# An mLSTM and mixer kernel: the first batch's weight staging, conversions and second token products put in another order

## The chip, the cores and the metric

The kernel runs on one core of one Trainium2 chip. Its engines are TensorE (PE; its weight loads are shown apart as PEld), VectorE (DVE), ScalarE (ACT), GpSimd (POOL) and SyncE (SP), which issues most of the DMAs. The metric is the device time of one execution in microseconds. TensorE's clock has two levels, 1.2 and 2.4 GHz; the profile shows the granted clock as a share of 2.4 GHz.

## The reference, cut to what matters

```python
for t in range(S):                      # B, H, S, D = 4, 8, 768, 40
    m_new = max(f[t] + m, i[t])
    f_stab, i_stab = exp(f[t] + m - m_new), exp(i[t] - m_new)
    C = f_stab * C + i_stab * outer(v[t], k[t])
    n = f_stab * n + i_stab * k[t]
    y[t] = sigmoid(o[t]) * (C @ q[t]) / max(abs(n . q[t]), 1)
x = y.transpose(0, 2, 1, 3).reshape(B, S, 320)
u = x + (relu(x^T @ w_tok1) @ w_tok2)^T     # token mixing: 768 -> 256 -> 768
out = u + relu(u @ w_ch1) @ w_ch2           # channel mixing: 320 -> 1536 -> 320
```

## The kernel before

The sequence is cut into NC = 6 chunks of 128 tokens; a unit is (batch, chunk). Within a chunk the recurrence becomes matrix products: scores `ps_sc` (`st_s`), weighted by exponentials `dd` (`prep_exp`, from a PSUM tile `ps_phi` for batch 0), times `v` (`st_pv`, tile `po`), plus the carried state `Cn` times the scaled queries `q3t` (`st_state`). `x0_ops` turns `po` into the mixer's input `x` and its two fp32r halves `xh`, `xl`.

The mixer's matmuls run in fp32r, each operand as a high and a low half. The weights come as 64-bit words in 30 pieces of 384 columns: pieces 0 to 3 are `w1`, 4 to 7 `w2`, then pairs of `c1` and `c2` in turn (8, 9 = `c1`; 10, 11 = `c2`; 12, 13 = `c1`; ...). A piece is loaded into a staged buffer `wst` (`dec_load`, SP). `dec_abs` makes its exponent part `pf` (ACT, in PSUM) and its low word (ACT, or GpSimd for even pieces once `early` is off). `dec_ops` joins them on DVE (two instructions a piece: `pf`, then `wf`). `dec_hi` (ACT) rounds `wf` to the high half, `dec_low` (GpSimd) subtracts for the low half. `wst` has four buffers in the pool `wq`, and three more in `wx` once `sp` is released.

Batch 0 goes chunk by chunk in a loop of five turns, c = 1 to 5; "turn 3" is the pass with c = 3, and u5 is the last unit of batch 0. Each turn does the scores of the next unit, the state and values of its own, and the decoding of two pieces. After the loop come the first token product (`a_part`, tile `ps_a`; `a_end` makes `rh`, `rl`), eleven small transposes of the gate sums (`cols`, tile `gt`, from `w_row`, which `rows_w` makes on GpSimd), the second token products (`phase_b`, six, tile `ps_b`), their transposes (`phase_t`, six), and then 18 slots: `gemm1` (16 products into `ps_h`; ACT makes `gh`, DVE `gl`) and, one slot late, `gemm2` (12 products into `acc`). Slots 0 to 10 of batch 0 also decode a pair of pieces each. Batches 1 to 3 follow with the attention of the next batch laced into the slots.

The order of instructions on each engine is the order of the code; semaphores set the rest. Every matmul of the mixer has one line, that of `mm3`, so stages are told apart by tiles. PSUM has eight banks: two each for `ps_h`, `acc`, `ps_s` and `ps_m`.

Of the kernel before, what the change touches and what calls it, by code (L numbers as in the profile page):

```python
# [25 lines left out]
HP = 9  # L26
# [8 lines left out]
def kernel(ctx: ExitStack, tc: tile.TileContext, gates, qk, q3, kv, og,  # L35
                            wt1, wt2, wc1, wc2, ident, out):
    nc = tc.nc
# [70 lines left out]
    floor_b = wp.tile([128, 1], F32, name="floor_b")  # L108
    nc.gpsimd.memset(floor_b, 2.0 ** -14 - 0.5)
    phi, b_t = z[0:B * HP, 0], z[0:B * HP, 1]  # L110
    w_row = pp.tile([B * HP, NC - 1, L], F32, name="w_row")
    phi_d = dp.tile([NC, B * HP, L], F32, name="phi_d")
    bcol = wp.tile([128, NC, B * HP], F32, name="bcol")
    wcol = wp.tile([128, NC, B * HP], F32, name="wcol")
# [28 lines left out]
                             t.rearrange("p (i g) -> p i g", i=3), AF.Exp)  # L143

    def rows_w():
        p = phi.rearrange("p (c t) -> p c t", t=L)[:, 0:NC - 1, L - 1:L]
        nc.gpsimd.tensor_tensor(w_row, b_t[:, 0:(NC - 1) * L].rearrange("p (c t) -> p c t", t=L),
                                p.to_broadcast([B * HP, NC - 1, L]), ALU.add)

    def cols():  # L150
        t = ps_m.tile([128, 2 * NC - 1, B * HP], F32, tag="m", name="gt")
        e = id_t[0:B * HP, 0:B * HP]
        for c in range(NC - 1):
            nc.tensor.transpose(t[:, c], w_row[:, c], e)
        for c in range(NC):
            nc.tensor.transpose(t[:, NC - 1 + c], b_t[:, c * L:(c + 1) * L], e)
        nc.scalar.activation(wcol[:, 0:NC - 1, :].rearrange("p c (b g i) -> p (c b) i g", b=B, g=3),
                             t[:, 0:NC - 1].rearrange("p c (b i g) -> p (c b) i g", b=B, g=3), AF.Exp)
        nc.vector.tensor_copy(bcol, t[:, NC - 1:])

    def spread_late(pool, tag):
        ps = pool.tile([128, 4, L], F32, tag=tag, name="ps_phi")
# [444 lines left out]
    def dec_load(n):  # L607
        while nxt[0] < min(n, len(pieces)):
            d, w, a = pieces[nxt[0]]
            late = wx and (nxt[0] - wx[1]) % 7 < 3  # L610
            t = (wx[0] if late else wq).tile([128, WP, 2], I32, tag="wst", name="wst", bufs=3 if late else 4)
            nc.sync.dma_start(out=t.rearrange("p n t -> p (n t)"), in_=w[:, a:a + WP].bitcast(I32))
            staged[nxt[0]] = t
            nxt[0] += 1
# [77 lines left out]
    def phase_b(b, s, pool=(ps_m, "m")):  # L692
        rh, rl = R[b]
        ps = pool[0].tile([128, DM], F32, tag=pool[1], name="ps_b")
        t = []
        for j in range(2):
            a = slice(j * S + s * 128, j * S + (s + 1) * 128)
            t += [(w2[0][:, a], rh[:, j, :]), (w2[1][:, a], rh[:, j, :]), (w2[0][:, a], rl[:, j, :])]
        mm3(ps, [t[i] for i in (0, 1, 3, 4, 2, 5)], True, True)
        x = xs[(b, s)][0]  # L700
        nc.vector.tensor_tensor(x, ps, x, ALU.add)
        xd = lp.tile([128, 2, 64], F32, tag="xd", name="xd", bufs=3)
        nc.vector.tensor_copy(xd, x[:, 256:320].unsqueeze(1).to_broadcast([128, 2, 64]))
# [51 lines left out]
    def step(g, n=1):  # L755
        for _ in range(n):
            next(g, None)

    def warm(n, pool=(ps_m, "m"), z=zero):
        t = pool[0].tile([128, 512], F32, tag=pool[1], name="warm")  # L760
        for i in range(n):
            nc.tensor.matmul(t[:, 0:z.shape[1]], z[:, 0:128], z, start=i == 0, stop=i == n - 1)

    us = units[:NC]
    xpool = {}
# [71 lines left out]
    for c in range(1, NC):  # L837
        u, n1, n2, n3 = (units[c + i] for i in range(4))
        if c == 1:
            st_s(n1)  # L840
        elif c < NC - 1:
            dg = dec_ops(0)
            st_s(n1, mid=dg)
        if c < 3:
            load_phi(n3)
            load_qk(n3, 0)
            load_qk(n3, 1)
        if c < NC - 1:
            spread_q(n1)
            prep_q3(n1)  # L850
            prep_kw(n1)
        if c == 1:
            dec_abs(2)
        st_state(u)
        if c == 1 or c == NC - 1:
            dg = dec_ops(0)
        if c < NC - 1:
            step(dg, 2 if c == 1 else 9)
        st_pv(u)
        if c < 4:  # L860
            load_kv(n2)
            load_q3(n2)
        dec_load(nxt[2] + 4)
        x0 = x0_ops(u)
        step(x0, 2)
        if c == 2:
            nc.sync.dma_start(out=phi_d.rearrange("c r t -> r c t"), in_=phi.rearrange("p (c t) -> p c t", t=L))
        if c < 4:
            spread_split(n2)
        if c == NC - 2:  # L870
            a_part(0, 0, 0)
            a_part(0, 1, 0)
        if c == 1:
            prep_exp(n2, 0)
            prep_exp(n2, 1)
            step(dg, 9)
        if c == NC - 1:
            step(x0, 9)
            step(dg, 9)
            rows_w()  # L880
        dec_hi()
        if 1 < c < 4:
            prep_exp(n2, 0)
            prep_exp(n2, 1)
        dec_low()
        dec_abs(nxt[2] + (2 if c < NC - 1 else 1))
        step(x0, 9)
        if c == 3:
            load_sig(1, 0)
        if c == 4:  # L890
            load_sig(1, 1)
    for i in range(1, NC - 1):
        a_part(0, 0, i)
        a_part(0, 1, i)
    ep.release()
    ss = (ps_s, "s")
# [6 lines left out]
    for b in range(B):  # L903
# [6 lines left out]
        if b:  # L910
            gemm2(*pend, half=0)
        if not b:
            warm(5, ss)
        for j in range(2):
            a_part(b, j, NC - 1)
            a_end(b, j)
# [17 lines left out]
        if b:  # L934
            slots = [(k, p) for k in range(3) for p in range(6)]
        else:
            sp.release()
            wx += [tc.alloc_tile_pool(name="wx", bufs=1, side="right"), nxt[0]]
            dec_load(nxt[0] + 3)
            pf = prep_first(units[NC], units[NC + 1])  # L940
            cols()
            pp.release()
            lp = ctx.enter_context(tc.tile_pool(name="lp", bufs=2))
            dec_abs(nxt[2] + 2)
            early[0] = False
            dg = dec_ops(0)
            phase_b(b, 0)
            phase_b(b, 1)
            phase_t(b, 0, ss)
            phase_b(b, 2)  # L950
            phase_t(b, 1, ss)
            phase_b(b, 3)
            phase_b(b, 4)
            step(dg, 9)
            dec_abs(nxt[2] + 2)
            slots = [(k, p) for p in range(6) for k in range(2)] + [(2, p) for p in range(6)]
        more = {1: [(phase_b, 4, ss)], 2: [(phase_t, 2, ss)], 4: [(phase_t, 3, ss)], 5: [(phase_b, 5)],
                9: [(phase_t, 4), (phase_t, 5, ss)]}
        for n, (k, p) in enumerate(slots):
# [96 lines left out]
```

## Time and profile before

| | |
|---|---|
| median of 3 runs | 443.0 us (441.61 to 443.83) |
| the profiled execution, and its span | 445.58 us, 443.9 us |
| PE busy, share of the span | 430.2 us, 97% |
| DVE, ACT, POOL busy | 300.8, 186.5, 137.2 us |
| mean granted clock | 0.992 |
| the chain that ended last | PE 88%, DVE 5%, issue 2%, DMA 2%, POOL 2% |

Times in the trace are microseconds from the span's start. The start of an instruction is firm; the end of a matmul is modelled, and matmuls overlap, so what a product costs is read from the distance between two starts. In brackets stands the idle time of the engine ahead of a row, and what ended it.

### The profile page before, as it was taken

How to read it: one execution, taken by the hardware profiler on the slowest of the kernel's cores; microseconds unless marked ns; L12 is line 12 of the kernel's file. 1: busy time of each engine (PE TensorE's matmuls, PEld its weight loads, DVE VectorE, ACT ScalarE, POOL GpSimd, SP SyncE). 2: the span in 40 equal slices, each digit the busy share in tenths (PEclk: the TensorE clock that was granted, in tenths of full speed). 3: DMA queues.
4: the chain of work that ended last, by engine and by line, in shares of the span. 5: the costliest groups of instructions: out<-in, count | busy, mean ns of one | idle time of the engine just before them, and what ended most of it. 6: DMA issues, size and time to landing. Idle time of an engine off the chain costs nothing.

```text
span 443.9 us, 9424 instructions
## 1 busy us (share of the span) xinstructions
PE 430.2 (97%) x3711; PEld 412.3 (93%) x3711; DVE 300.8 (68%) x669; ACT 186.5 (42%) x424; POOL 137.2 (31%) x175
## 2 busy tenths in 40 slices
PE   8987987999999999999999999999999999999997
PEld 4776887999999999999999999999999999999996
DVE  8997777672677669699886878698886736233212
ACT  6866555786445464342332354442332312112111
POOL 7474615674164450403422330403422110000000
PEclk9999988999999999999999999999999999999999
DMA  7967456960487743231753423231530000000000
GB/s 214 276 195 262 138 179 186 327 197 2 135 234 214 236 157 98 89 88 50 219 155 98 138 63 103 85 97 45 177 106 31 1 2 30 1 17 14 8 25 30
DMA packets 24576, 52.37 MB, mean 118 GB/s; under 512 B 2565, under 2 KB 13325, under 8 KB 24533
## 3 DMA queue, kind: packets, MB, share of 16 engines
q1 hardware_dynamic: 24293, 51.61, 37.9%
q8 instruction: 29, 0.48, 0.5%
q10 hardware_dynamic: 240, 0.18, 0.2%
q14 instruction: 14, 0.11, 0.1%
HBM read 47.73 MB, written 4.04 MB: 117 GB/s over the span
## 4 chain that ended last, share of the span: by engine, by line
PE 88%; DVE 5%; issue 2%; DMA 2%; POOL 2%; ACT 1%; SPq 0%; DVEq 0%; POOLq 0%; ACTq 0%
PE ps_h L668 31%; PE acc L668 29%; PE ps_b L668 5%; PE ps_sc L308 5%; PE ps_a L668 4%; PE po L424 4%; PE po L398 3%; PE pu L376 2%; PE po L403 2%; PE po L368 1%; DMA wst<-in_wt_dram 1%; PE ps_t L715 1%; PE ps_t L717 1%; PE ps_t L716 1%; DVE m_t L120 1%
## 5 line engine op out<-in xcount | busy, mean ns | idle before, releaser
L668 PE MATMUL ps_h<-uT,c1h 128*128 128x256 f32 x720 | 141.3, 284 | 0.9 <-ACT c1h L656 0.9
L735 ACT ACTIVATE gh<-ps_h 128x512 fp32r<-128x512 f32 x72 | 43.0, 597 | 187.1 <-PE ps_h L668 187.1
L668 PEld LDWEIGHTS ps_h<-uT,c1h 128*128 128x128 f32 x720 | 116.4, 190 | 1.8 <-ACT c1h L656 1.1
L668 PE MATMUL ps_h<-uT,c1l 128*128 128x256 f32 x432 | 112.4, 282 | 0.7 <-POOL c1l L662 0.7
L736 DVE SCALAR_TENSOR_TENSOR gl<-ps_h,gh 128x512 fp32r<-128x512 f32 x72 | 49.6, 689 | 90.3 <-ACT gh L735 89.9
L668 PE MATMUL acc<-c2h,gh 128*128 128x320 f32 x288 | 90.6, 322 | 0.0
L668 PE MATMUL acc<-c2l,gh 128*128 128x320 f32 x288 | 86.9, 309 | 0.0
L668 PEld LDWEIGHTS ps_h<-uT,c1l 128*128 128x128 f32 x432 | 82.0, 190 | 0.9 <-POOL c1l L662 0.9
L668 PE MATMUL acc<-c2h,gl 128*128 128x320 f32 x288 | 65.5, 308 | 0.0
L668 PEld LDWEIGHTS acc<-c2h,gh 128*128 128x128 f32 x288 | 54.4, 189 | 1.3
L668 PEld LDWEIGHTS acc<-c2l,gh 128*128 128x128 f32 x288 | 54.3, 189 | 0.0
L668 PEld LDWEIGHTS acc<-c2h,gl 128*128 128x128 f32 x288 | 48.1, 188 | 0.0
L443 POOL TENSOR_TENSOR sig<-sig,ht 128x320 f32<-128x320 f32 x18 | 14.8, 821 | 107.2 <-DVE ht L406 100.8
L289 ACT ACTIVATE dd<-dd,bcol 128x128 f32<-128x128 f32 x144 | 45.7, 391 | 0.6 <-POOL dd L279 0.6
L318 DVE TENSOR_TENSOR dd<-ps_sc,dd 128x512 f32<-128x512 f32 x48 | 30.9, 680 | 1.5 <-PE ps_sc L308 1.5
L494 POOL TENSOR_TENSOR xl<-x,xh 128x320 fp32r<-128x320 f32 x18 | 15.8, 877 | 47.5 <-DVE xh L492 46.2
L308 PE MATMUL ps_sc<-raw 64*128 64x128 f32 (+1 forms) x384 | 28.5, 285 | 0.0
L308 PEld LDWEIGHTS ps_sc<-raw 64*128 64x128 f32 (+1 forms) x384 | 23.7, 187 | 4.2 <-issue 2.5
L279 POOL TENSOR_SCALAR_AFFINE_SELECT dd<-dd 128x1024 f32<-128x1024 f32 x18 | 22.1, 1229 | 4.4 <-DMA dd<-phi_d 2.7
L424 PE MATMUL po<-kvt,dd 128*128 128x41 f32 (+1 forms) x192 | 23.2, 277 | 0.0
L331 DVE TENSOR_TENSOR r<-dd 128x512 f32<-128x512 f32 x24 | 22.6, 980 | 0.0
L424 PEld LDWEIGHTS po<-kvt,dd 128*128 128x128 f32 x192 | 22.4, 192 | 0.1
(145 smaller groups left out, 761.8 us busy)
## 6 DMA issues: line engine op xcount, KB each, us to landing
dd<-phi_d SPq DMA_DIRECT2D x18, 512.0 KB
wst<-in_wc_dram SPq DMA_DIRECT2D x22, 384.0 KB
kvt<-in_kv_dram SPq DMA_DIRECT2D x24, 324.0 KB
raw<-in_qk_dram SPq DMA_DIRECT2D x48, 160.0 KB
sig<-in_og_dram SPq DMA_DIRECT2D x8, 480.0 KB
out_dram<-x SPq DMA_DIRECT2D x24, 160.0 KB
q3t<-in_q_dram SPq DMA_DIRECT2D x20, 180.0 KB
wst<-in_wt_dram SPq DMA_DIRECT2D x8, 384.0 KB
```

What stands on the lines that cost most here:

```text
L279: nc.gpsimd.affine_select(dd, dd, pattern=[[0, H], [1, L]], compare_op=ALU.is_ge, fill=-1e30, base=0, channel_multiplier=-1)
L289: nc.scalar.activation(dd[:, h, :], dd[:, h, :], AF.Exp, bias=bcol[:, c, HP * b + h:HP * b + h + 1])
L308: nc.tensor.matmul(t["s"][hf][:, h, :], r[:, 1, h, :], r[:, 0, h, :], start=True, stop=True)
L318: nc.vector.tensor_tensor(dd, t["s"][hf], dd, ALU.mult)
L331: nc.vector.tensor_tensor(r[:, h], dd[:, h], top(dd)[:, h], ALU.subtract)
L398: nc.tensor.matmul(po[:, h - h0, 0:j1 - j0], p[i][:, ROW[h], :], w[:, h, j0:j1], start=h == h0 and i + j0 == 0, stop=c == 0 and h == h1 - ...
L424: nc.tensor.matmul(o, t["dd"][:, ROW[h], :], x, start=c == 0 and h == 0, stop=h == H - 1)
L443: nc.gpsimd.tensor_tensor(sg, sg, ht[:, :, 0:D], ALU.mult)
L494: nc.gpsimd.tensor_tensor(xl, x, f32(xh), ALU.subtract)
L668: nc.tensor.matmul(ps, a, m, start=(first and i == 0), stop=(last and i == n - 1))
L735: nc.scalar.activation(gh, ps, AF.Relu)
L736: nc.vector.scalar_tensor_tensor(gl, ps, 0.0, f32(gh), op0=ALU.max, op1=ALU.subtract)
```

## The change

- Pieces 4, 5, 8 and 9 are staged in two buffers of their own, in the pool `ep`; `dec_load` runs ahead of the next unit's `kvt` and `q3t` loads and by a fixed count, 2c + 4.
- In turns 2 and 3 the exponentials of the next unit stand ahead of the conversions on ACT.
- `w_row` is made in turn 4 (`c == NC - 2`) ahead of `prep_q3`. `bcol` is copied by ACT, not DVE. The copies `xd` of batch 0 are GpSimd's.
- Pieces 8 to 11 get their exponent and low parts at the end of turn 4; pieces 8 and 9 are joined after the loop.
- The filler of five bf16 products ahead of the last first token product becomes two fp32r products of 512 columns.
- All six second token products and four transposes stand ahead of slot 0; two of them ran after slot 0's `gemm1`, with one second token product. The products 2 to 5 use the `acc` banks.

```diff
     def rows_w():
+        xpool[3] = w_row = ep.tile([B * HP, NC - 1, L], F32, name="w_row")
...
-        nc.vector.tensor_copy(bcol, t[:, NC - 1:])
+        nc.scalar.activation(bcol, t[:, NC - 1:], AF.Copy)
...
-            late = wx and (nxt[0] - wx[1]) % 7 < 3
-            t = (wx[0] if late else wq).tile([128, WP, 2], I32, tag="wst", name="wst", bufs=3 if late else 4)
+            k = nxt[0]
+            pool, n_b = (xpool[2], 2) if k in (4, 5, 8, 9) else (wx[0], 3) if wx and (k - wx[1]) % 7 < 3 else (wq, 4)
+            t = pool.tile([128, WP, 2], I32, tag="wst", name="wst", bufs=n_b)
...
-        nc.vector.tensor_copy(xd, x[:, 256:320].unsqueeze(1).to_broadcast([128, 2, 64]))
+        (nc.vector if b else nc.gpsimd).tensor_copy(xd, x[:, 256:320].unsqueeze(1).to_broadcast([128, 2, 64]))
...
+        if c == NC - 2:
+            rows_w()
...
         st_pv(u)
+        dec_load(2 * c + 4)
         if c < 4:
             load_kv(n2)
             load_q3(n2)
-        dec_load(nxt[2] + 4)
...
         if c < 4:
             spread_split(n2)
+            prep_exp(n2, 0)
+            prep_exp(n2, 1)
...
+        if c < NC - 1:
             step(dg, 9)
-            rows_w()
-        dec_hi()
-        if 1 < c < 4:
-            prep_exp(n2, 0)
-            prep_exp(n2, 1)
-        dec_low()
-        dec_abs(nxt[2] + (2 if c < NC - 1 else 1))
+            dec_hi()
+            dec_low()
+            if c == NC - 2:
+                dec_abs(nxt[2] + 2)
+                step(x0, 9)
+                early[0] = False
+            dec_abs(nxt[1] + 2)
...
-            warm(5, ss)
+            warm(2, z=w1[0][:, 0:512])
...
-            dec_load(nxt[0] + 3)
             pf = prep_first(units[NC], units[NC + 1])
             cols()
+            ep.release()
...
-            dec_abs(nxt[2] + 2)
-            early[0] = False
-            dg = dec_ops(0)
+            aa = (ps_acc, "acc")
+            step(dg, 9)
+            dec_load(nxt[2] + 7)
+            dg = dec_ops(9)
             phase_b(b, 0)
             phase_b(b, 1)
-            phase_t(b, 0, ss)
-            phase_b(b, 2)
-            phase_t(b, 1, ss)
-            phase_b(b, 3)
-            phase_b(b, 4)
+            dec_hi()
+            dec_low()
+            phase_b(b, 2, aa)
+            phase_b(b, 3, aa)
+            step(dg, 1)
+            phase_t(b, 0)
+            phase_t(b, 1)
+            phase_b(b, 4, aa)
+            phase_b(b, 5, aa)
+            step(dg, 1)
+            phase_t(b, 2)
+            phase_t(b, 3)
             step(dg, 9)
+            dec_hi()
+            dec_low()
             dec_abs(nxt[2] + 2)
...
                 if n == 0:
-                    phase_t(b, 2)
-                    phase_t(b, 3)
-                    phase_b(b, 5)
-                    dec_hi()
-                    dec_low()
                     step(dec_ops(9), 9)
```

On SP, in turn 3, these are the loads for the last unit (`kvt_632`, `q3t_634` before; `kvt_635`, `q3t_637` now) and those of pieces 8 and 9 (the first two `wst` from `in_wc1`). Before:

```order
L867 DMA phi_d_136<-z_100 36x6x128
L242 DMA kvt_632<-in_kv_dram 128x648
L253 DMA q3t_634<-in_q3_dram 120x384
L612 DMA wst_637<-in_wc1_dram 128x768
L612 DMA wst_639<-in_wc1_dram 128x768
```

And now:

```order
L613 DMA wst_631<-in_wc1_dram 128x768
L613 DMA wst_633<-in_wc1_dram 128x768
L242 DMA kvt_635<-in_kv_dram 128x648
L253 DMA q3t_637<-in_q3_dram 120x384
L54 DMA sig_679<-in_og_dram 128x3x320
```

The two weight pieces moved ahead of the unit's own loads.

On ACT, around the first two slots (`gh` is a slot's result, `c1h` and `c2h` are conversions, `uT` the evictions of the transposes). Before:

```order
L718 ACTIVATE uT<-ps_t 128x3x128 x2
L623 ACTIVATE pf<-wst 128x384 x2
L627 ACTIVATE wst<-wst,floor_b 128x384
L735 ACTIVATE gh<-ps_h_951 128x512
L718 ACTIVATE uT<-ps_t 128x3x128 x2
L656 ACTIVATE c2h<-wf 128x384 x2
L623 ACTIVATE pf<-wst 128x384 x2
L627 ACTIVATE wst<-wst,floor_b 128x384
L656 ACTIVATE c1h<-wf 128x384 x2
L735 ACTIVATE gh<-ps_h_1043 128x512
```

And now:

```order
L719 ACTIVATE uT<-ps_t 128x3x128 x4
L657 ACTIVATE c2h<-wf 128x384 x2
L624 ACTIVATE pf<-wst 128x384 x2
L628 ACTIVATE wst<-wst,floor_b 128x384
L736 ACTIVATE gh<-ps_h_985 128x512
L624 ACTIVATE pf<-wst 128x384 x2
L628 ACTIVATE wst<-wst,floor_b 128x384
L657 ACTIVATE c1h<-wf 128x384 x2
L736 ACTIVATE gh<-ps_h_1040 128x512
```

The conversions `c2h` of pieces 10 and 11 moved from behind slot 0's `gh` to ahead of it, and with them the parts of pieces 12 and 13.

On GpSimd, in turn 4 (`w2l` are the low halves of pieces 4 to 7, `xl` that of turn 3's `x`, `q3t` the scaled queries of u5). Before:

```order
L476 TENSOR_TENSOR xl<-x,xh 128x320
L275 TENSOR_TENSOR q3t<-q3t,pq 120x384
L662 TENSOR_TENSOR w2l<-wf,w2h 128x384 x2
L476 TENSOR_TENSOR xl<-x,xh 128x320
L147 TENSOR_TENSOR w_row<-z 36x640
```

And now:

```order
L476 TENSOR_TENSOR xl<-x,xh 128x320
L147 TENSOR_TENSOR w_row<-z 36x640
L275 TENSOR_TENSOR q3t<-q3t,pq 120x384
L663 TENSOR_TENSOR w2l<-wf,w2h 128x384 x2
L476 TENSOR_TENSOR xl<-x,xh 128x320
```

`w_row` moved ahead of `q3t`.

## Rows read from the trace of the kernel before

**Rows 1.** Busy time by stretch: length, PE, PEld, DVE, ACT, POOL, clock, DMA.
```profile
57.00:62.00 5.00, 5.00 (x25) 4.68 (x24) 3.45 (x9) 1.51 (x4) 0.54 (x1) 0.66 0.92 336
...
74.50:78.50 4.00, 3.95 (x19) 3.95 (x20) 2.56 (x6) 2.56 (x7) 3.73 (x5) 0.57 0.99 255
78.50:108.00 29.50, 29.50 (x228) 29.50 (x227) 17.22 (x32) 23.76 (x52) 19.80 (x23) 1.00 0.60 187
```

**Rows 2.** Waits of PE from 26 to 82 us: total, times, longest.
```profile
PE ps_b L668 <- ACT c2h L656: 1.7, 1, 1.7
...
PE ps_q L196 <- ACT dd L286: 1.3, 1, 1.3
```

**Rows 3.** Timeline of ACT, turns 2 and 3: start, length, instruction.
```profile
31.32 0.99 ACT L656 ACTIVATE w1h<-wf 128x384 fp32r<-128x384 f32 x2 [1.91 <-DVE wf L644]
32.21 1.07 ACT L286 ACTIVATE dd<-ps_phi 128x512 f32<-128x512 f32 x2
35.40 0.52 ACT L623 ACTIVATE pf<-wst 128x384 f32<-128x384 f32 x1 [2.11 <-DMA wst<-in_wt_dram]
```

**Rows 4.** Timeline of SP's DMA issues.
```profile
30.17 1.99 SPq L612 DMA_DIRECT2D wst<-in_wt_dram  x4
...
36.84 0.43 SPq L253 DMA_DIRECT2D q3t<-in_q_dram  x1
...
54.77 17.97 SPq L612 DMA_DIRECT2D wst<-in_wc_dram  x9
```

**Rows 5.** Timeline of DVE, turn 3.
```profile
36.51 0.57 DVE L641 SCALAR_TENSOR_TENSOR pf<-pf,wst 128x384 int32<-128x384 int32 x1 [2.58 <-ACT wst L627]
...
39.59 1.01 DVE L644 SCALAR_TENSOR_TENSOR wf<-wst,pf 128x384 int32<-128x384 int32 x2
```

**Rows 6.** Timeline of POOL, turn 4 to the second token products.
```profile
45.34 1.02 POOL L275 TENSOR_TENSOR q3t<-q3t,pq 120x384 f32<-120x384 f32 x1
...
50.99 1.26 POOL L147 TENSOR_TENSOR w_row<-z 36x640 f32<-36x640 f32 x1
...
58.23 0.54 POOL L629 TENSOR_SCALAR wst<-wst 128x384 int32<-128x384 uint16 x1 [1.64 <-DMA wst<-in_wc_dram]
```

**Rows 7.** Timeline of PE from turn 5 to slot 2.
```profile
46.41 0.95 PE L368 MATMUL po<-Cn,q3t 120*128 120x164 f32 x6 [0.36 <-POOL q3t L275]
...
52.55 1.25 PE L762 MATMUL warm<-zero 128*128 128x512 bf16 x5
53.45 0.50 PE L668 MATMUL ps_a<-xh,w1h 128*128 128x320 f32 x1
...
56.37 0.41 PE L668 MATMUL ps_b<-rh,w2h 128*128 128x320 f32 x1 [0.89 <-ACT rh L685]
...
62.55 0.31 PE L668 MATMUL ps_b<-rh,w2h 128*128 128x320 f32 x1
...
63.43 0.28 PE L668 MATMUL ps_h<-uT,c1h 128*128 128x256 f32 x1
...
65.32 0.27 PE L715 MATMUL ps_t<-id_t,x 128*128 128x128 f32 x1
...
74.55 0.39 PE L668 MATMUL ps_h<-uT,c1l 128*128 128x256 f32 x1 [0.70 <-POOL c1l L662]
```

**Rows 8.** Timeline of DVE around slots 0 and 2.
```profile
62.39 0.42 DVE L719 TENSOR_TENSOR uT<-ps_t,uT 128x256 fp32r<-128x256 f32 x1
...
63.17 0.49 DVE L701 TENSOR_TENSOR x<-ps_b,x 128x320 f32<-128x320 f32 x1
...
69.96 1.02 DVE L641 SCALAR_TENSOR_TENSOR pf<-pf,wst 128x384 int32<-128x384 int32 x2
```

**Rows 9.** The page's costliest groups: busy, mean ns, idle before.
```profile
L735 ACT ACTIVATE gh<-ps_h 128x512 fp32r<-128x512 f32 x72 | 43.0, 597 | 187.1 <-PE ps_h L668 187.1
...
L736 DVE SCALAR_TENSOR_TENSOR gl<-ps_h,gh 128x512 fp32r<-128x512 f32 x72 | 49.6, 689 | 90.3 <-ACT gh L735 89.9
```

**Rows 10.** Groups of POOL, shapes apart.
```profile
L91 POOL CAST late_b<-late 128x128 bf16<-128x128 f32 x1 | 0.3, 289 | 0.1
```

More of the change, by code (lines that the diff above doesn't have):

```diff
@@ L110 @@
     phi, b_t = z[0:B * HP, 0], z[0:B * HP, 1]
-    w_row = pp.tile([B * HP, NC - 1, L], F32, name="w_row")
     phi_d = dp.tile([NC, B * HP, L], F32, name="phi_d")
@@ L153, in cols @@
         for c in range(NC - 1):
-            nc.tensor.transpose(t[:, c], w_row[:, c], e)
+            nc.tensor.transpose(t[:, c], xpool[3][:, c], e)
         for c in range(NC):
@@ L761, in warm @@
         for i in range(n):
-            nc.tensor.matmul(t[:, 0:z.shape[1]], z[:, 0:128], z, start=i == 0, stop=i == n - 1)
+            nc.tensor.matmul(t[:, 0:z.shape[-1]], z[:, 0:128], z, start=i == 0, stop=i == n - 1)
     us = units[:NC]
@@ L854 @@
         st_state(u)
-        if c == 1 or c == NC - 1:
+        if c == 1:
             dg = dec_ops(0)
@@ L872 @@
             a_part(0, 1, 0)
-        if c == 1:
-            prep_exp(n2, 0)
-            prep_exp(n2, 1)
+        if c < NC - 1:
             step(dg, 9)
-        if c == NC - 1:
-            step(x0, 9)
-            step(dg, 9)
-            rows_w()
-        dec_hi()
-        if 1 < c < 4:
-            prep_exp(n2, 0)
-            prep_exp(n2, 1)
-        dec_low()
-        dec_abs(nxt[2] + (2 if c < NC - 1 else 1))
+            dec_hi()
[5 more added lines that the diff above has]
+            dec_abs(nxt[1] + 2)
         step(x0, 9)
@@ L891 @@
             load_sig(1, 1)
+    ss = (ps_s, "s")
+    dg = dec_ops(0)
+    step(dg, 2)
     for i in range(1, NC - 1):
@@ L894 @@
         a_part(0, 1, i)
-    ep.release()
-    ss = (ps_s, "s")
     pend = None
```

## The prediction

> **What bounds the kernel now.** I read the page first: PE is busy for 97% of the span and the chain that ended last is 88% PE, so a change that takes no work from PE can gain only where PE stands idle or runs slow. The 40 slices say where: PE falls below nine tenths only in the first eight, up to about 80 us. The busy time by stretch then shows what the stretches cost [rows 1]. From 78.5 to 108 us PE is busy for 29.50 of 29.50 us at full clock; ACT, with 23.76, is the next fullest. In two stretches the granted clock sags: 0.66 over 57 to 62 us and 0.57 over 74.5 to 78.5, each losing about 1.7 us of full speed (0.34 x 5, 0.43 x 4). The list of PE's waits and its timeline give the gaps: 1.7 for a second token product that ran after slot 0's products, 1.3 for exponentials [rows 2], 0.36 at turn 5's state product, 0.89 at the first second token product, 0.70 at slot 2 [rows 7].
>
> Each wait has a weight piece behind it. In turn 2 ACT converts pieces 2 and 3 first (0.99 us) and makes the exponentials after (1.07) [rows 3], while PE waits for them. In turn 3 ACT waits 2.11 us for piece 4 to land [rows 3], since SP issued its load at 30.17 [rows 4], and DVE waits 2.58 us in consequence [rows 5]. At slot 2, PE waits for piece 12's low half.
>
> **The change part by part.** PE's work is nearly the same: five bf16 filler products go, two fp32r ones come. The rest is order, so I follow the path that ends last and mark it at five starts in the trace of before: turn 5's state product 46.41, the last first token product 53.45, the first second token product 56.37, slot 0 63.43, and slot 2's second product 74.55 [rows 7].
>
> Turns 2 to 4. Pieces 4 and 5 have buffers of their own and are asked for in turn 1, several us earlier, so ACT's 2.11 us and DVE's 2.58 [rows 3, 5] go; I take 2.6. The exponentials ahead of the conversions fill idle time of ACT in turn 3, and no longer stand between its conversions and what follows, which gives GpSimd's `xl` another 1.0 of the 1.07 [rows 3]. So `q3t`, 45.34 before [rows 6], would start at 45.34 - 2.6 - 1.0 = 41.7. What is late next stands on its own engine: `w_row` now runs ahead of it, 1.26 [rows 6], and it starts at 43.0. It lasts 1.02, so the state product comes at 44.1 instead of 46.41: a gain of 2.3.
>
> The transfer. The load of u5's `q3t`, issued at 36.84 before [rows 4], now stands on SP behind those of pieces 8 and 9, which wait until DVE has joined 4 and 5: 39.59 + 1.01 - 2.6 = 38.0 [rows 5]. SP issues four weight loads in 1.99 [rows 4], about 0.5 each, so `q3t` leaves at about 38.8. A piece issued into idle queues at 54.77 was waited for until 58.23 [rows 4, 6], 3.5 us; the first of four pieces issued at 30.17, behind other loads, until 35.40 [rows 3, 4], 5.2 us. So `q3t` lands between 42.3 and 44.0. I take 43.1, the middle, which `w_row` all but hides; the upper end costs 0.9.
>
> The Trainium skill ("DMA: Bandwidth & Descriptors", section "Queues, rings and completion order") speaks against this edit: each DMA engine takes the descriptors of a ring in their order, so `q3t` stands behind the whole of both pieces. The 5.2 us above agrees, and the late landing is a rival below.
>
> Turn 5 to the first second token product. Between 46.41 and 53.45 lie 7.04 us, of which the old filler took 0.90 (52.55 to 53.45) [rows 7]. A product of 320 columns follows the one before after 0.147 (six in 62.55 to 63.43) [rows 7], so two of 512 cost about 0.48, an estimate by columns; the ends are 0.3 and 0.9. 44.1 + 7.04 - 0.90 + 0.48 = 50.7. From there to 56.37 were 2.92 us with 0.89 of waiting for `rh` [rows 7], which stood on ACT behind a weight piece's parts; these now come before it. 50.7 + 2.0 = 52.7: 3.6 gained.
>
> Second token products and slots 0 and 1. Six products of 0.88 make 5.3; twelve transposes, at no more than the 0.118 of a slot's product (16 in 63.43 to 65.32) [rows 7], make 1.4 or less, I take 1.3. Slot 0 starts at 52.7 + 6.6 = 59.3, 4.1 before its old place, with a second token product and two pairs of transposes already behind it, and slot 1 ends at 63.1. The sag at 57 to 62 us [rows 1], which followed the 0.89 gap, I count as gone.
>
> Then much of it is given back, since weights 10 to 13 haven't kept pace. On DVE the joining of pieces 10 and 11 ends behind the fourth transpose's eviction. The fourth second token product ends at 52.7 + 3.5 = 56.2; its addition ends 0.7 later, at 56.9. Then DVE has two `pf` (1.02), four pairs of evictions at 0.78 (62.39 to 63.17) and two additions at 0.49 [rows 8]: 5.1, so `wf` starts at 62.0 and the first is there at 62.5. Now ACT runs, in this order, two conversions (0.99 [rows 3]), two `pf` (0.52 each [rows 3], overlapping a little: 0.9), a low half (I put it at 0.6, a little over a `pf`), and only then slot 0's `gh`: 65.0, though its products ended at 61.2. `gh` takes 0.60 and DVE's `gl` 0.69, 0.1 less with overlap [rows 9]; only then come `pf` of pieces 12 and 13, at 66.1. Before, that started at 69.96 [rows 8]. From it to slot 2's second product passed 4.59 (69.96 to 74.55) [rows 7, 8], through the same instructions in the same order. So that product starts at 70.7, 3.9 early, and PE has by then stood idle for some 5 us in two pieces. The clock falls here as it did before [rows 1]: the 1.7 stays.
>
> Hidden edits. `bcol` costs ACT some 0.4 before the second product, which PE fills with the first; without that cover, 0.4. The six `xd` copies leave DVE for GpSimd. The nearest row is a cast of the same shape, 0.29 [rows 10]; the ends are 0.2 and 1.26 (`w_row`'s [rows 6]). At 0.29 they lie beside PE's products; at 1.26 the third and fourth would hold the transposes back by about 2. Slots' later pieces: their loads move with the decoding, so nothing is gained or lost.
>
> The sum is 3.9. After slot 2 PE has the same work in both. The profiled execution took 445.58, 1.7 more than its span of 443.9; less 3.9 is 441.7. It ran 2.6 above the median of 443.0, and against that median I forecast 439.1.
>
> **The rivals.**
>
> *The slots don't wait.* If ACT reaches slot 0's `gh` in time, PE alone sets the path: slot 1 ends at 63.1, `gemm2` takes 1.8 (12 x 0.147), slot 2 starts at 64.9, and its second product is over 9 us early. Half of that shortfall already makes the gain 7: 436. For it: ACT has idle time around 60. Against: 62.5 needs no bad luck, only DVE's twelve instructions in order.
>
> *The loads land late and the clock falls there too.* `q3t` at 44.0 takes 0.9, and PE, idle for two us, then runs turn 5 at the lower level, 1.2 GHz, as it ran slow after 0.89 of idle time before [rows 1, 7]: another 1.7. The gain shrinks to 1.3: 441.7. By the Trainium skill's ring order, named above, this is where the change pays.
>
> *Decoding sets the pace of the slots: slower.* From slot 0's `gh` to slot 1's pass, by the chain above, 5.2 us (`gl`, two `pf`, two `wf`, the next parts, conversions), against PE's 16 x 0.118 + 12 x 0.147 = 3.65 a slot. I hold that this happens once: the `pf` of the pair after next is then made while DVE works, and ACT needs 0.60 + 0.9 + 0.6 + 0.99 = 3.1 a slot. If the chain instead holds at ScalarE's `gh` in every decoding slot, each costs 1.5. It has eaten the 3.9 after the third and decides from there; five slots give 443.0 - 3.9 + 7.5 = 446.6, all ten 454. Against it: the 29.50 of 29.50 us that PE is busy in these slots now [rows 1].
>
> *Little changes.* Both stalls at the slots are longer than I think by two each: 443.
>
> **How the numbers follow.** The forecast has 0.50 (437.5 to 440.8), slots that don't wait 0.15 (433 to 437.5), late loads 0.20 (440.5 to 442.3), little change 0.06, decoding as the pace 0.09 (above 445). A measurement of this kernel can tell about 0.5% from no change, 2.2 us. Below 440.8 lie the forecast, the slots that don't wait and half of the late loads: 0.75. Within are the other half and the little change, 0.16. Above, 0.09. The range 435.0 to 442.3 leaves out a third of the second case and the last two: about 0.2.
>
> **What would show it.** Right, step by step: no ACT wait on a weight DMA in turn 3; turn 5's state product near 44.1, with GpSimd's `w_row` ending just ahead of `q3t`; the first second token product near 52.7 with no wait; no sag of the clock around 57 us; slot 0 near 59.3; then two waits of PE, for ACT's `gh` (about 2) and for `c1l` (about 3), and a sag after them; slot 2's second product near 70.7, and the same work after it. Wrong: a GpSimd wait for the `q3t` DMA past 44; a sag in turn 5; `gh` following slot 0's products at once; or slots after the second that still wait for `gh` or `c1l`.

## The result, and the profile after

The changed kernel took 447.01 us, median of 20 runs (442.60 to 450.13), against 442.96 for the kernel before; the ratio is 1.0073, 95% interval 1.0048 to 1.0097. It is slower by 0.7%, about 3 us by this ratio and 4.05 between the two medians, where 439.1 was forecast. The ratios, here and below, are of fast runs: two of the changed kernel's 20 (449.4 and 450.1 us) and a few stray ones, among them one of e3_both at 2348 us that its range leaves out too, are not in them. The profiled execution took 448.39 us with a span of 446.7 (before: 445.58 and 443.9). From 100 us on both keep PE busy at full clock but for 0.1 us, so all of it happens in the first 100 us.

The runs scatter with the clock that TensorE was granted over the span: 442.6 us where its mean was 0.996, 443.4 and 443.9 at 0.992, 448.4 to 450.1 at 0.977. The kernel before has such a spread too, a smaller one: of its 29 runs beside the first experiments, those at 0.999 or 1.0 took 441.8 to 443.4 us and the eight at 0.992 took 444.5 to 445.8. Its profiled execution was one of the latter.

TensorE first (timeline: start, duration, line, operation, tiles and shapes, count, and in brackets the idle time before it and what ended it); these answer to [rows 7]:

```profile
33.68 0.95 PE L368 MATMUL po<-Cn,q3t 120*128 120x164 f32 x6 [1.80 <-POOL q3t L275]
...
41.22 0.90 PE L368 MATMUL po<-Cn,q3t 120*128 120x164 f32 x6
...
46.95 0.95 PE L368 MATMUL po<-Cn,q3t 120*128 120x164 f32 x6 [1.51 <-POOL q3t L275]
...
56.68 0.31 PE L669 MATMUL ps_a<-xh,w1h 128*128 128x320 f32 x1
...
58.45 0.41 PE L669 MATMUL ps_b<-rh,w2h 128*128 128x320 f32 x1
...
65.12 0.36 PE L669 MATMUL ps_h<-uT,c1h 128*128 128x256 f32 x1
...
71.03 0.41 PE L669 MATMUL acc<-c2h,gh 128*128 128x320 f32 x1 [1.89 <-ACT gh L736]
75.15 0.58 PE L669 MATMUL ps_h<-uT,c1h 128*128 128x256 f32 x1 [1.16 <-ACT c1h L657]
76.24 0.58 PE L669 MATMUL ps_h<-uT,c1l 128*128 128x256 f32 x1 [0.51 <-POOL c1l L663]
```

The waits for `rh`, `c2h` and `dd` [rows 2, 7] are gone. New are the first line, a wait in turn 3 of which the prediction says nothing, and the longer waits of turn 5 and the slots. GpSimd's timeline shows whom turn 3 waits for; it answers to [rows 6]:

```profile
32.63 1.00 POOL L275 TENSOR_TENSOR q3t<-q3t,pq 120x384 f32<-120x384 f32 x1 [2.71 <-DMA q3t<-in_q_dram]
37.68 1.00 POOL L275 TENSOR_TENSOR q3t<-q3t,pq 120x384 f32<-120x384 f32 x1 [0.50 <-DMA q3t<-in_q_dram]
44.67 1.26 POOL L147 TENSOR_TENSOR w_row<-z 36x640 f32<-36x640 f32 x1
45.89 1.00 POOL L275 TENSOR_TENSOR q3t<-q3t,pq 120x384 f32<-120x384 f32 x1
```

Turn 3's `q3t` came about 32.6 us. SP's queue shows when it was asked for, and behind what [rows 4]:

```profile
20.49 1.60 SPq L613 DMA_DIRECT2D wst<-in_wt_dram  x2
23.26 0.33 SPq L242 DMA_DIRECT2D kvt<-in_kv_dram  x1
23.72 0.35 SPq L253 DMA_DIRECT2D q3t<-in_q_dram  x1
...
27.06 1.21 SPq L613 DMA_DIRECT2D wst<-in_wt_dram  x2
```

Pieces 4 and 5 (2 x 384 KB) leave ahead of it; from its issue to its use pass 8.9 us. In the kernel before only `kvt` was issued just ahead of it, and GpSimd's multiply waited for nothing:

```profile
30.00 1.00 POOL L275 TENSOR_TENSOR q3t<-q3t,pq 120x384 f32<-120x384 f32 x1
```

The waits of the changed kernel themselves add up to 6.9 us, but they replace others. What they do to the clock is in the busy time by stretch (length, busy time of each engine with the number of instructions, then PEclk, DMA share and GB/s), beside [rows 1]:

```profile
35.00:40.00 5.00, 5.00 (x35) 4.38 (x33) 3.92 (x13) 0.60 (x1) 3.87 (x6) 0.70 0.28 68
...
45.00:50.00 5.00, 3.48 (x22) 3.22 (x22) 3.01 (x9) 3.87 (x9) 4.30 (x5) 0.82 1.04 385
50.00:55.00 5.00, 5.00 (x21) 5.00 (x21) 2.97 (x8) 1.32 (x3) 0.92 (x2) 0.50 0.10 39
55.00:60.00 5.00, 5.00 (x38) 4.68 (x38) 2.22 (x5) 2.26 (x6) 0.00 (x0) 1.00 0.21 48
...
70.00:75.00 5.00, 2.96 (x12) 2.42 (x12) 3.40 (x7) 2.80 (x6) 1.78 (x3) 0.71 0.50 151
75.00:80.00 5.00, 4.34 (x18) 4.05 (x19) 3.75 (x8) 3.35 (x9) 4.52 (x6) 0.50 1.00 332
80.00:85.00 5.00, 5.00 (x32) 5.00 (x31) 2.65 (x5) 3.00 (x7) 3.06 (x4) 0.77 1.03 361
```

After each group of waits PE runs at 0.50, the lower of its two levels (1.2 GHz). Full speed lost: 0.30 x 5 = 1.5 us in turn 3, 0.9 + 2.5 = 3.4 in turn 5, 1.5 + 2.5 + 1.2 = 5.1 at the slots, 10.0 in all, against about 3.5 in the profile of before. That is 6.5 us more, on a span only 2.8 longer. Not all of it lies on the path that ends last; what does is read from the marks further down. A busy PE is no proof of progress: 50 to 55 us is 5.00 of 5.00 busy, with 21 products.

### The profile page after: what moved, and what is told of

It is laid out like the page before. It is cut to its first block, busy times and chain, and to the rows that moved or that the text cites. A ratio compares the mean times of both kernels' runs of the same rounds, so it can differ in the third digit from the quotient of the medians.

```text
span 446.7 us, 9423 instructions
## 1 busy us (share of the span) xinstructions
PE 435.0 (97%) x3708; PEld 417.5 (93%) x3708; DVE 298.5 (67%) x662; ACT 186.6 (42%) x424; POOL 137.9 (31%) x182
## 4 chain that ended last, share of the span: by engine, by line
PE 82%; issue 1%; DVE 0%; ACT 0%; POOL 0%; POOLq 0%; DVEq 0%
PE ps_h L669 30%; PE acc L669 29%; PE ps_sc L308 5%; PE ps_b L669 4%; PE ps_a L669 4%; PE po L398 3%; PE po L424 2%; PE pu L376 2%; PE po L403 2%; PE po L368 1%; PE ps_t L718 0%; PE ps_t L716 0%; PE ps_t L717 0%; DVE pf L642 0%; POOL c1l L663 0%
## 5 line engine op out<-in xcount | busy, mean ns | idle before, releaser
L424 PE MATMUL po<-kvt,dd 128*128 128x41 f32 (+1 forms) x192 | 25.6, 295 | 0.0
L424 PEld LDWEIGHTS po<-kvt,dd 128*128 128x128 f32 x192 | 24.8, 209 | 0.1
```

Of the source, the lines that this page charges most:

```text
L424: nc.tensor.matmul(o, t["dd"][:, ROW[h], :], x, start=c == 0 and h == 0, stop=h == H - 1)
```

## The experiments

Each was timed beside the kernel before. "Changed" is the kernel predicted; clock is the median over the runs of the mean granted clock.

| run | edit | us | lowest to highest | ratio to before, 95% | clock |
|---|---|---|---|---|---|
| changed | | 447.01 | 442.6 to 450.1 | 1.0048 to 1.0097 | 0.986 |
| e1_loads | changed, pieces behind `kvt`, `q3t` | 441.40 | 439.9 to 442.4 | 0.9940 to 0.9982 | 0.995 |
| e11_turn1 | the same in turn 1 alone | 445.15 | 442.2 to 449.3 | 1.0008 to 1.0073 | 0.987 |
| e14_turn13 | the same but for turn 2 | 441.34 | 440.0 to 444.1 | 0.9950 to 0.9996 | 0.994 |
| e12_queue | changed, pieces 4, 5 on ScalarE's queue | 445.68 | 442.8 to 448.9 | 1.0021 to 1.0080 | 0.988 |
| e13_wrow | changed, row sums behind `q3t` | 445.10 | 441.8 to 448.1 | 1.0016 to 1.0075 | 0.988 |
| e3_both | e1 + row sums behind `q3t` | 438.75 | 438.6 to 439.0 | 0.9871 to 0.9939 | 0.995 |
| e7_fill | changed + zero products, turns 3, 5 | 443.44 | 441.5 to 447.0 | 0.9987 to 1.0045 | 0.994 |
| e15_t1_fill5 | e11 + zero products, turn 5 | 443.31 | 442.4 to 444.5 | 0.9977 to 1.0017 | 0.996 |
| e4_gh | changed, conversions behind `gh` | 444.05 | 442.6 to 445.4 | 1.0002 to 1.0046 | 0.990 |
| e6_slots | changed, slots as before | 444.86 | 441.4 to 447.8 | 1.0011 to 1.0068 | 0.988 |
| e5_all | e3 + conversions behind `gh` | 438.02 | 437.8 to 438.4 | 0.9863 to 0.9916 | 0.999 |
| e9_slots | e3, slots as before | 438.59 | 438.3 to 439.5 | 0.9879 to 0.9934 | 0.998 |
| e8_exps | e3, exponentials as before | 441.30 | 439.8 to 443.7 | 0.9937 to 0.9985 | 0.996 |
| e10_fill_gh | e5 + zero products at slot 0 | 437.99 | 437.8 to 438.2 | 0.9852 to 0.9902 | 1.000 |

**The order of the loads.** In every turn:

```
         st_pv(u)
-        dec_load(2 * c + 4)
         if c < 4:
             load_kv(n2)
             load_q3(n2)
+        dec_load(2 * c + 4)
```

> The changed kernel with one edit: in every turn the two weight pieces are issued behind the next unit's kvt and q3t, as in the kernel before, not ahead of them. Theory (three late places, each followed by a stretch at the half clock; the first is turn 3's q3t, which waits 2.71 us on POOL for its transfer and makes the state product wait 1.80 us): POOL's multiply of q3t in turn 3 stands near 30.0 us without a wait on a DMA (after the change 32.63), turn 3's state product at or before 33.1 (33.68), the half-clock stretch at 34.8 to 38 is gone, turn 5's state product stands at 44 to 45 (46.95), and the time falls by 2 to 3 us, to 444 to 445. Rival A (the loss lies at the slots alone, 1.89 + 1.16 + 0.51 us of waits and the half clock from 72.5 to 82): the early part moves ahead, the slots run into the same waits or longer ones, and the time stays within 1 us of 447.0. Rival B (the pieces, now later, stop the conversions instead): ACT waits for a piece in turn 2 or 3, and the time does not fall.

It gave 441.40, 5.6 us less than the changed kernel, twice what the theory asked for. Rivals A and B fall (from 20 to 45 us ACT waits for no piece). GpSimd's timeline of e1_loads:

```profile
29.84 1.01 POOL L275 TENSOR_TENSOR q3t<-q3t,pq 120x384 f32<-120x384 f32 x1
```

and PE's:

```profile
31.63 0.93 PE L368 MATMUL po<-Cn,q3t 120*128 120x164 f32 x6
...
38.43 0.90 PE L368 MATMUL po<-Cn,q3t 120*128 120x164 f32 x6
...
44.13 0.95 PE L368 MATMUL po<-Cn,q3t 120*128 120x164 f32 x6 [1.18 <-POOL q3t L275]
...
50.74 0.31 PE L669 MATMUL ps_a<-xh,w1h 128*128 128x320 f32 x1
...
52.52 0.41 PE L669 MATMUL ps_b<-rh,w2h 128*128 128x320 f32 x1
...
59.19 0.37 PE L669 MATMUL ps_h<-uT,c1h 128*128 128x256 f32 x1
...
70.30 0.38 PE L669 MATMUL ps_h<-uT,c1l 128*128 128x256 f32 x1 [0.70 <-POOL c1l L663]
```

`q3t` is used at 29.84 without a wait and turn 3's product comes 2 us earlier; the clock is 1.00 from 25 to 65 us. Which turn matters was not what I thought:

> The changed kernel with the weight pieces behind kvt and q3t in turn 1 alone (pieces 4 and 5); in turn 2 and later they stay ahead. Theory (turn 3's q3t, issued in turn 1 behind pieces 4 and 5, is the one that matters; turn 4's waited 0.50 us on POOL): 441 to 442.5, as with all turns (441.4). Rival (the pieces of turn 2 do the same to turn 4's q3t, or what counts is the amount that is under way at 27 to 33 us and not the order): 443.5 or more, with a wait of turn 4's state product or of POOL on its q3t.

445.15: the rival's time, by neither's mechanism. Turn 3's and turn 4's products stand as in e1_loads, but turn 5's waits 3.04 us. PE and SP's queue in e11_turn1:

```profile
46.09 0.95 PE L368 MATMUL po<-Cn,q3t 120*128 120x164 f32 x6 [3.04 <-POOL q3t L275]
```

```profile
37.46 0.83 SPq L613 DMA_DIRECT2D wst<-in_wc_dram  x2
38.39 0.37 SPq L242 DMA_DIRECT2D kvt<-in_kv_dram  x1
38.81 0.43 SPq L253 DMA_DIRECT2D q3t<-in_q_dram  x1
```

SP holds pieces 8 and 9 until their buffers, those of 4 and 5, are free, with u5's `kvt` and `q3t` behind them; in e1_loads that `q3t` left earlier:

```profile
36.31 0.43 SPq L253 DMA_DIRECT2D q3t<-in_q_dram  x1
```

In e11_turn1 the profile puts GpSimd's wait for it, until 45.03, down to ScalarE's `pf`, which the multiply doesn't read. In e12_queue, with the same order in turn 3, it names the DMA (in e15_t1_fill5 too, until 44.87):

```profile
45.32 1.00 POOL L275 TENSOR_TENSOR q3t<-q3t,pq 120x384 f32<-120x384 f32 x1 [2.12 <-DMA q3t<-in_q_dram]
```

In the changed kernel the row sums, which end at 45.9, hide this landing. Then:

> The changed kernel with the weight pieces behind kvt and q3t in turns 1 and 3 (and after), ahead of them in turn 2 alone. Theory (two places count, one behind the other: turn 1's order delays turn 3's q3t, turn 3's delays turn 5's, where SP also waits for the staging buffers of pieces 4 and 5; turn 2's order costs nothing): 440.8 to 442, as with all turns (441.4), no wait on a DMA at POOL's q3t multiplies, turn 5's state product near 44.1. Rival (turn 2's order is part of the loss, through turn 4's q3t): 443 or more, and a wait at turn 4's q3t.

441.34, the theory's, with turn 5's product nearly where e1_loads has it:

```profile
44.23 0.95 PE L368 MATMUL po<-Cn,q3t 120*128 120x164 f32 x6 [1.17 <-POOL q3t L275]
```

Turn 4's `q3t` did wait on GpSimd for its DMA, 1.58 us, against the theory's word, but PE did not wait for it. So two places count, turn 1's order for turn 3 and turn 3's for turn 5, and the first hides the second. Turn 3's order mended alone was not run.

> The changed kernel with pieces 4 and 5 issued by ScalarE ahead of turn 2's exponentials instead of by SP ahead of kvt and q3t; order of everything else as in the changed kernel. Theory (q3t is late because it stands behind 768 KB in SP's queue): POOL's wait of 2.71 us for turn 3's q3t falls under 1 us, and the time to 441 to 443.5. Rival (the transfers share the same engines, whose share is 0.9 to 1.1 at 27 to 33 us, so that it doesn't matter which queue the pieces are in): the same wait of 2 us or more and a time of 445.5 or more; or ScalarE's issue delays the exponentials, which would show as a wait for dd.

The edit: `(nc.scalar if k in (4, 5) else nc.sync).dma_start(...)` in `dec_load`. It separates the two halves of the delay. ScalarE issued the pieces at 20.45 and 21.08, as early as SP had, and GpSimd's wait for turn 3's `q3t` fell from 2.71 to 1.04 us and PE's to 0.21. So place in the queue was 1.67 us of the 2.71; that the remaining 1.04 comes from sharing the DMA engines is argued, not shown. The theory's time was missed, since turn 5's wait, 3.33 us, came out as in e11_turn1. The ring order that the prediction cites from the Trainium skill ("DMA: Bandwidth & Descriptors", "Queues, rings and completion order") agrees with the first half.

**The row sums.** `rows_w()` in turn 4 moves behind `prep_kw(n1)`, so behind `q3t`.

> The changed kernel with two edits: the weight pieces behind kvt and q3t, and the row sums (w_row, 1.26 us on POOL) behind turn 4's q3t multiply and key weights instead of ahead of them. Theory: beside what the load order gives, turn 5's state product no longer waits 1.51 us for q3t; it stands 1 to 1.3 us earlier than in the kernel with the load order alone, the half clock from 48.6 to 55 is shorter or gone, and the time is 442 to 443.5, 1 to 2 us under the load order alone. Rival A (slots alone): within 1 us of 447.0. Rival C (turn 5 is set by another engine than POOL, so that w_row ahead of q3t costs nothing): the same time as the load order alone within 0.7 us, and turn 5's state product waits for something else.

438.75, where the theory had 442 to 443.5. Turn 5's product stands at 42.96 with no wait (44.13 in e1_loads); 1.2 us of work order became 2.65 us of time (2.2 between the profiled spans). Where the rest comes from is in e3_both's rows at slot 2,

```profile
69.14 0.39 PE L669 MATMUL ps_h<-uT,c1l 128*128 128x256 f32 x1 [0.71 <-POOL c1l L663]
```

and in its stretches:

```profile
65.00:70.00 5.00, 3.46 (x17) 2.86 (x16) 4.10 (x9) 3.93 (x9) 1.93 (x2) 0.73 0.56 183
70.00:75.00 5.00, 5.00 (x41) 5.00 (x40) 4.08 (x9) 4.16 (x10) 3.86 (x6) 1.00 0.99 302
```

beside e1_loads':

```profile
70.00:75.00 5.00, 4.70 (x24) 4.71 (x25) 3.71 (x8) 3.84 (x10) 4.29 (x6) 0.66 0.97 308
```

Slot 2's second product comes 1.16 us earlier (69.14 against 70.30). The other 1.0 lies behind it: e1_loads runs there at the lower clock, while e3_both's low stretch falls ahead of that product, among waits for other engines. Alone:

> The changed kernel with one edit: the row sums (w_row) behind turn 4's q3t multiply and key weights, the loads as in the changed kernel. Theory (the two places add up: 2.7 us of the 8.3 between the changed kernel and the one with both edits): 443.5 to 445.5, turn 3's wait for q3t and the half clock after it stay, turn 5's wait of 1.51 us goes. Rival (turn 5's wait only shows because turn 3 came late, and is worth nothing by itself): 446.3 or more. The other rival (the row sums are the main cause): 442.5 or less.

445.10, in the theory's range, but its interval overlaps the changed kernel's: beside turn 3's wait the row sums cannot be priced well.

**Wait or clock.** Zero products multiply tiles of zeros into the group of products that waits: they keep PE busy and add nothing to the sums. In `st_state`, ahead of the three state products:

```
+            fill = {3: 10, 5: 8}.get(c, 0) if x else 0
+            for i in range(fill):
+                nc.tensor.matmul(pof[:, 0:(x + H) * E1], zero[:, 0:128],
+                                 zero[:, 0:(x + H) * E1], start=i == 0, stop=False)
```

> The changed kernel, its order untouched, with zero products (bf16, 369 columns) on TensorE just ahead of the state products of turns 3 (10 of them) and 5 (8): they fill PE's waits of 1.80 and 1.51 us for q3t and add nothing to the sums. Theory (a large part of the loss is not the two waits themselves but the half clock after them): the state products stand where they stood (33.7 in turn 3), the stretch at the half clock that follows turn 3's wait and the one from 48.6 to 55 are gone, the mean clock rises from 0.977 to 0.985 or more, and the time falls by 2 to 4 us, to 443 to 445. Rival (the waits themselves are the loss, the clock falls anyhow): the same low stretches, and a time within 1 us of 447.0.

443.44, with the clock up from 0.986 to 0.994: the theory's numbers. But in the profiled execution turn 3's `q3t` happened to land sooner (POOL waited 0.44 us), so this run alone could not tell the two apart. The clean one fills a wait that stands still, with `{5: 18}` on e11_turn1:

> The changed kernel with the pieces behind kvt and q3t in turn 1 alone (445.15 us without the filling; turn 5's state product waits 3.04 us for q3t, and the granted clock is 0.74 and 0.58 over 45 to 50 and 50 to 55), and 18 zero products (bf16, 369 columns) ahead of turn 5's state product. Theory (the half clock is about half of the cost of such a wait): the state product stays at 46 us, the clock is full from 45 to 55, and the time falls by 1.5 to 3.5 us, to 441.7 to 443.7. Rival (the wait itself is the cost, the clock falls anyhow or costs nothing): within 1 us of 445.15.

443.31, as the theory had it: 1.8 us less with the state product where it was. The stretches of e11_turn1:

```profile
45.00:50.00 5.00, 3.91 (x23) 3.91 (x24) 0.58 (x2) 3.48 (x7) 4.28 (x5) 0.74 0.90 334
50.00:55.00 5.00, 5.00 (x22) 5.00 (x22) 2.97 (x8) 0.47 (x1) 0.00 (x0) 0.58 0.01 4
```

and of e15_t1_fill5, with its zero products and the state product behind them:

```profile
45.00:50.00 5.00, 4.94 (x38) 4.39 (x37) 1.72 (x7) 3.48 (x7) 4.15 (x5) 1.00 0.95 356
50.00:55.00 5.00, 5.00 (x40) 4.67 (x39) 3.17 (x8) 1.88 (x5) 0.00 (x0) 1.00 0.12 20
```

```profile
42.88 2.99 PE L368 MATMUL po<-zero 128*128 128x369 bf16 x18
45.93 0.95 PE L371 MATMUL po<-Cn,q3t 120*128 120x164 f32 x6
```

Same start (45.93 against 46.09), full clock, 40 products in place of 22 from 50 to 55 us. Slot 0 then starts 3.3 us earlier, first e11_turn1, then e15_t1_fill5:

```profile
64.28 0.37 PE L669 MATMUL ps_h<-uT,c1h 128*128 128x256 f32 x1
```

```profile
60.98 0.36 PE L672 MATMUL ps_h<-uT,c1h 128*128 128x256 f32 x1
```

From the state product to slot 0 pass 18.2 us at the lower clock and 15.05 with it full (15.06 in e1_loads). So beside a wait of 3.04 us the half clock after it cost 3.1 in this execution and 1.8 in the median, whose run had a higher clock than the profiled one (0.987, 0.981). The profiled spans, 446.0 and 441.3, lie 4.7 apart, since the low stretch at the slots is longer in e11_turn1 as well.

**The slots.** `dec_hi()`, `dec_low()` of the second pair move behind slot 0's `gemm1`; in e6_slots and e9_slots `phase_t` of blocks 2, 3 and `phase_b` of block 5 too.

> The changed kernel with one edit: the second pair's conversions and differences (c2h 68.13 us, c2l) stand behind slot 0's gh instead of ahead of it, as in the kernel before. Theory: gh of slot 0 stands about 1.5 to 2 us earlier (after the change 70.41), PE's wait of 1.89 us for it falls under 0.5, c1h and c1l come later, so that slot 2 waits for them as long as now or up to 1 us longer (1.16 + 0.51 after the change); the time falls by 0.5 to 1.5 us, to 445.5 to 446.5, and the half clock at 72.5 to 82 is shorter. Rival A (slots alone are the loss): the time falls by 3 us or more, to 444 or less. Rival D (decoding paces the slots whatever the order): the wait moves from gh to c1h and c1l in full, and the time stays within 0.5 us of 447.0.

> The changed kernel with one edit: the transposes of token blocks 2 and 3, the second token product of block 5 and the second pair's conversions stand behind slot 0's first products, as in the kernel before, so that not all second token products are ahead of the slots. Theory: slot 0 starts 1.5 to 2 us earlier than after the change, gh is not late, the work behind it fills PE while c1h and c1l are made, and the waits at 71 to 76 us (1.89 + 1.16 + 0.51) fall under 2 us in all; the early half-clock stretches at 34.8 to 38 and 48.6 to 55 stay; time 445 to 446. Rival A (slots alone are the loss): 444 or less, as fast as the kernel before or faster. Rival D (decoding paces the slots whatever the order): within 0.5 us of 447.0.

444.05 and 444.86, below the theory's ranges and above rival A's 444; in e4_gh PE waits 1.4 for `c2h` and 1.1 for `c2l` instead of 1.9 for `gh`, and the clock is 1.00 from 70 to 85 us. With the early places mended:

> Three edits to the changed kernel: weight pieces behind kvt and q3t, row sums behind turn 4's q3t multiply (these two gave 438.75 us), and the second pair's conversions behind slot 0's gh. Theory (with the early stalls gone, PE's wait of 1.9 us for gh at slot 0 is the largest left on the path, at 62 to 65 us, and a half-clock stretch follows it): gh moves 1 to 1.5 us ahead, c2h and c2l are late instead by part of it; the time falls by 0.3 to 1.5 us, to 437.2 to 438.5. Rival (decoding paces the slots): the wait only changes its name, from gh to c2h and c2l, and the time stays at 438.4 to 439.1.

> The kernel with both edits (438.75 us), with another part of the change undone: the transposes of token blocks 2 and 3, the second token product of block 5 and the second pair's conversions stand behind slot 0's first products again. Theory (all second token products ahead of the slots gain little, since slot 0 then only starts later and gh, c1h and c1l are late instead of the c2h of before): the time within 1 us of 438.75, between 438 and 439.8, with a wait for uT at block 5's second product (2.8 us in the changed kernel with the same edit) in place of that for gh. Rival (that part is a gain of its own, as the prediction's 0.7 us at this place has it): 439.8 or more; the opposite rival (it is a loss of its own): 438 or less.

438.02 and 438.59 against 438.75: the order at the slots is worth 0.7 us and nothing. Rival A of e1_loads, e3_both, e4_gh and e6_slots, that the slots alone are the loss, falls with e3_both, which leaves them as they are.

> The fastest kernel so far (pieces behind kvt and q3t, row sums behind q3t, the second pair's conversions behind gh: 438.02 us) with 12 zero products of 320 columns ahead of the first products of acc, where PE waits 1.4 us for c2h. Theory (the half-clock stretch at 65 to 70 us, granted clock 0.66 there, follows this wait): the stretch goes, and the time falls by 0.5 to 1.5 us, to 436.5 to 437.5. Rival (c2h and the decoding pace this stretch, so that PE only waits longer at the full clock): within 0.4 us of 438.0; if the zero products delay PE, up to 1 us more.

437.99, the rival's: the clock is 1.00 throughout, and nothing is gained over e5_all, most of whose runs had 0.999 anyway. The low stretch of e5_all's profiled execution (0.66 from 65 to 70 us) lay among waits for other engines: slot 2's second product came 10.3 us after slot 0 with it and without. With e5_all this is the fastest kernel here, 1.2% under the kernel before.

**What the change is worth in itself.** In e8_exps turns 2 and 3 have the exponentials behind the conversions again.

> The kernel with both edits (pieces behind kvt and q3t, row sums behind q3t: 438.75 us), with one part of the change undone: in turns 2 and 3 the next unit's exponentials stand behind the conversions again. Theory (the exponentials ahead of the conversions took away PE's wait for dd, 1.3 us before, and the later start of the second turn): turns 3 and 4 start 0.5 to 1.3 us later, DVE's or PE's wait for dd comes back, and the time rises by 0.5 to 2 us, to 439.3 to 440.8. Rival (the gain of the change comes from the pieces that are there a turn sooner and the work at the slots; the exponentials only move a wait): within 0.5 us of 438.75.

441.30, 2.55 us more, beyond the theory's upper end. PE's waits in e8_exps, between 20 and 110 us (total, times, longest):

```profile
PE ps_q L196 <- ACT dd L286: 1.3, 1, 1.3
PE ps_q L196 <- DVE den L467: 0.7, 1, 0.7
```

The first is that of [rows 2] again. By this one undoing, the exponentials are the larger part of the 4.2 us that e3_both is faster than the kernel before.

## Why the prediction was wrong

Its path, mark by mark (us; e1_loads is the changed kernel with its loads in the old order):

| mark | before | forecast | changed | e1_loads |
|---|---|---|---|---|
| turn 5's state product | 46.41 | 44.1 | 46.95 | 44.13 |
| last first token product | 53.45 | 50.7 | 56.68 | 50.74 |
| first second token product | 56.37 | 52.7 | 58.45 | 52.52 |
| slot 0 | 63.43 | 59.3 | 65.12 | 59.19 |
| slot 2's second product | 74.55 | 70.7 | 76.24 | 70.30 |

The chain was right, to 0.4 us, for a kernel whose `q3t` is on time. The changed kernel and e1_loads part by 2.05 us at turn 3's state product (33.68, 31.63), by 0.7 more at turn 4's (41.22, 38.43), by nothing more at turn 5's, by 3.1 more up to slot 0, by nothing up to slot 2's second product, and by 1.3 behind it (spans 446.7 and 439.5). The first is the late `q3t`; 0.7, 3.1 and 1.3 are stretches in which PE is busy and the changed kernel runs at the lower clock for longer. From slot 0 to slot 2's second product pass 11.1 us in both, and before: PE waits there for ACT and GpSimd, and the half clock of the changed kernel from 72 to 76 us costs nothing. Two steps failed, and a rival was sized too small.

*"Pieces 4 and 5 have buffers of their own and are asked for in turn 1, several us earlier, so ACT's 2.11 us and DVE's 2.58 [rows 3, 5] go."* They go; the changed kernel has no such wait. But the step gave the earlier load its gain alone. In turn 1 it is also put ahead of u3's `kvt` and `q3t`, 768 KB in front of a transfer that was needed at 30 us. The prediction followed just this for u5's `q3t` in turn 3 and not for turn 1, two turns sooner. Mending both turns is worth 5.6 us, and e11_turn1 and e14_turn13 show that they are the whole of it.

*The rival "the loads land late and the clock falls there too"* had the mechanism, its page and the place (turn 5), with a chance of 0.20, and was sized too small. In e11_turn1, where it stands alone, `q3t` was multiplied at 45.03, later than the 44.0 that the rival took as the latest; PE stood idle for 3.04 us where it had two, and the clock lost 1.3 + 2.1 = 3.4 where it had 1.7. Against e1_loads that is 3.75 us; the rival had 0.9 + 1.7 = 2.6. The upper end for the landing, 44.0, came from a piece with only `kvt` and `q3t` just ahead of it (SP issued them at 29.24 and 29.63 us in the kernel before); here two pieces and `kvt` stood ahead.

*"It ran 2.6 above the median of 443.0, and against that median I forecast 439.1."* The 3.9 counted the 1.7 of the sag at 57 to 62 us as gone. But the profiled execution had a mean clock of 0.992, and 17 of the 29 runs of before named above had 0.999 or 1.0, so that its median has little of such a loss to give back. e1_loads, with every mark as forecast, took 441.19 profiled (the forecast's sum before it was carried to the median: 441.7) and 441.40 in the median: 2.3 above 439.1. This and the 5.6 make the 7.9.

The rest held: `w_row` ahead of `q3t` (1.26), `xd` copies on GpSimd at 0.29 to 0.30, no wait for `rh`, no sag at 57 to 62. Slot 0's `gh` came at 64.47 in e1_loads (65.0), in the changed kernel at 70.41, behind just the work that the prediction lists; ScalarE's timeline there, beside [rows 3]:

```profile
68.13 0.99 ACT L657 ACTIVATE c2h<-wf 128x384 fp32r<-128x384 f32 x2 [2.23 <-DVE wf L645]
69.02 0.92 ACT L624 ACTIVATE pf<-wst 128x384 f32<-128x384 f32 x2
69.89 0.62 ACT L628 ACTIVATE wst<-wst,floor_b 128x384 int32<-128x384 uint16 x1
70.41 0.57 ACT L736 ACTIVATE gh<-ps_h 128x512 fp32r<-128x512 f32 x1
```

The rival of decoding as the pace of every slot had nothing for it: from 85 to 90 us PE is busy for 5.00 of 5.00 us at full clock in the changed kernel and in e1_loads.

## What to carry to other kernels

A prefetch that is moved ahead has a price on its queue: list every load that it now stands in front of, turn by turn, with the time at which each is needed, and do so again after mending the first, since one late load hides the next. Take a gain against the profiled execution's own clock: what that execution lost to a low clock, the median run may not have lost. A wait at TensorE can cost about twice its length where work of its own follows: in e11_turn1 a state product 1.9 us later than in e14_turn13 cost 3.8, of which products that add nothing gave back 1.8. Where PE then waits for other engines anyway, as at the slots, a low clock costs nothing and a filler gains nothing.

## What the runs showed of the hardware

- The same waits can be followed by low stretches of different lengths. At the slots the changed kernel waits 1.89, 1.16 and 0.51 us and runs at 0.50 from about 72 to 82.3; e1_loads waits 1.9, 1.9 and 0.7 there and is at 0.50 from 71 to about 74.4. What makes the difference stays open. It is part of why e4_gh gains 3.0 us on the changed kernel and the same edit 0.7 on e3_both: from 70 us on e3_both was at full clock already.
- Waits of 1.17 us (turn 5 in e14_turn13) and of 1.3 and 0.7 us (e8_exps) left the clock at 1.00, and so did 1.48 and 1.69 in the kernel before (at 41.69 and 67.83 us); 1.51 us in the changed kernel's turn 5 did not, nor 0.89 before. The length of one wait alone does not decide it.
- How soon a load lands differs between runs of one order: with pieces 4 and 5 ahead of it turn 3's `q3t` was waited for until 32.2 to 32.6 us in four profiled executions and until 30.3 in e7_fill, where SP had issued these pieces at 18.69 instead of 20.5 to 20.7.
